# Issuing the first value columns of a fused attention and gated feed-forward kernel from the first attention result, with the value products one step earlier

## The chip, the cores and the metric

The kernel runs on one core of a Trainium2 chip. The metric is the device time of one execution in microseconds (us); the kernel before was run four times, and its median is 254.11 us. A traced execution gives the profile; all times of events below are counted from the start of that execution's span.

The engines are named as in the profile: PE is TensorE's matmul, PEld its weight load, DVE is VectorE, ACT is ScalarE, POOL is GpSimd, SP is SyncE. DMA transfers are issued by GpSimd (queue q0 in the profile) or by SyncE (queue q1), and both are carried by the same 16 DMA engines of the core.

## What is computed

The reference is an attention followed by a gated feed-forward. Batch 4, 8 heads, 768 positions, head size 64; the feed-forward goes from 512 to 1536 columns and back.

```python
scores = scale * q @ k.T + bias            # bias: -slope(head) * distance
keep = (key < 8) | ((query >= key) & (query - key < 96))
a = softmax(where(keep, scores, -1e9))
x = (a @ v)                                # heads side by side: 3072 rows of 512
out = (relu(x @ w_gate) * (x @ w_val)) @ w_out
```

Each query sees 8 global keys and at most 96 keys before it, so only a narrow band of the scores is computed.

## The kernel before

The work is cut into eight parts `s` = 0 to 7, each half a sequence (384 queries) of one batch item. For each part the attention writes `xT` (the result, transposed, 4 pieces of 128 rows, one for each pair of heads `p`), and the feed-forward of that part follows. It has 12 groups `fc` of hidden columns: `gate(fc)` makes four products with `wg` (L487) and a relu, `val(fc)` makes four products with `wv` (L500), and VectorE multiplies both (L502) into `ht`. Then `outp` multiplies `ht` by `wo_sb` (L521).

The weights come in blocks of four groups: `wg[0]`, `wv[0]` serve groups 0 to 3, and so on. In HBM they are float32; the transfers that GpSimd issues (L172, called by `load_gate` and `load_val`) convert them to bfloat16 on the way. Queries and keys come as float32 through SyncE (L131), in transfers of two heads each for parts 0 and 1: keys, then queries, for pairs 0, 1, 2, 3.

The order of the work is written out by hand: every engine runs its instructions in the order in which the Python code issues them. Parts 0 and 1 are handled apart from the others. For a pair `p` of part 1 the steps are:

- `piece_cast(1, p)` (L243 to L254): keys and queries to bfloat16, two instructions at L252 on the engine that `copy` names;
- `T(p)`, `piece_t` (L275): six transposes on TensorE (L283), then VectorE's evictions to `qT` (L288) and `kT` (L271 to L273);
- `BI(p, g)`, `piece_bias` (L336): the bias products of one of two PSUM groups;
- `SC(p, g)`, `piece_score` (L353): the score products added on top, then ScalarE's exponent (L358);
- `AW(p)`, `piece_av_wide` (L433): sums and attention products, ScalarE's logarithm and exponent (L439, L441), VectorE's product into `xT` (L444).

The list that `attention_pieces(1, fill)` returns (L465 to L468) sets their order on TensorE, and `f[0]` to `f[7]` are groups of the feed-forward of part 0 placed between them: `val(0)` to `val(3)`, `gate(4)`, `gate(5)`, `val(4)`, `val(5)`. Ahead of this list TensorE runs `gate(0)` to `gate(3)`; between the second and the third of these `piece_cast(1, 1)` is put into ScalarE's queue.

The score groups take turns in two PSUM buffers, so `BI` of a pair waits until the exponent of the pair before has read the same buffer. GpSimd's order in this stretch is at L561 to L581: memsets, `piece_cast(1, 0)`, `load_val(0)`, `load_v_half(1)` (the rest of the value rows of the first batch item, L155), `piece_cast(1, 2)`, `load_gate(1)`, memsets, `load_val(1)` and so on. In the kernel before, `piece_cast(1, 3)` is run by VectorE at the place of `C(3)` in the list of L465.

Of the kernel before, what the change touches and what calls it, by code (L numbers as in the profile page):

```python
# [15 lines left out]
def kernel(  # L16
# [12 lines left out]
    nc = tc.nc  # L29
# [82 lines left out]
    wv = [const.tile([128, N_DC, GW * 128], BF16, name=f"wv{i}") for i in range(N_FC // GW)]  # L112
# [27 lines left out]
    def load_v_globals(b):  # L140
        nc.gpsimd.dma_start(out=v_dst(b, 0, NG, 0),
                            in_=v[b, :, 0:NG, :].rearrange("h p d -> p h d"))
# [28 lines left out]
    def load_w(dst, src, f0, f1):  # L171
        nc.gpsimd.dma_start(out=dst, in_=src[:, f0:f1].rearrange("(c p) f -> p c f", p=128))  # L172

    def load_gate(i):
        load_w(wg[i], moe_w_gate, i * GW * 128, (i + 1) * GW * 128)

    def load_val(i):
        load_w(wv[i], moe_w_val, i * GW * 128, (i + 1) * GW * 128)
# [58 lines left out]
    xT_of = {}  # L237
# [5 lines left out]
    def piece_cast(s, p):  # L243
        qk = cast_pool.tile([128, 2, NN, 2, D], BF16, name="qk")
        cast_of[s, p] = qk
        for i, src in ((1, ks_of[s]), (0, qs_of[s])):
            copy = nc.gpsimd.tensor_copy
            if s == 0:
                copy = (nc.vector.tensor_copy, nc.scalar.copy, nc.scalar.copy, nc.vector.tensor_copy)[p]
            elif s == 1 and p % 2 == 1:  # L250
                copy = (nc.scalar.copy, nc.vector.tensor_copy)[p // 2]
            copy(  # L252
                qk[:, i].rearrange("t n e d -> t e n d"),
                src[:, 2 * p : 2 * p + 2, :].rearrange("t e (n d) -> t e n d", n=NN))  # L254
# [20 lines left out]
    def piece_t(s, p):  # L275
        b, half = divmod(s, 2)
        kt = kT[b % 2][p]
        qk = cast_of[s, p]
        tp = av_psum.tile([128, 512], FP32, name="av_ps")
        tp = tp[:, 0:QH].bitcast(BF16).rearrange("d (i t) -> d i t", i=2)  # L280
        for i in range(2):
            for n in range(NN):
                nc.tensor.matmul(tp[:, i, n * 128 : (n + 1) * 128],  # L283
                                 lhsT=qk[:, i, n],
                                 rhs=ident, is_transpose=True,
                                 start=(i == 0 and n == 0), stop=(i == 1 and n == NN - 1))
        if s < 2:
            nc.vector.tensor_copy(qTb[s][:, p, 0, :], tp[:, 0, :])  # L288
        else:
            for e in range(2):  # L290
                r = slice(64 * e, 64 * e + 64)
                nc.vector.tensor_copy(qTb[s % 2][r, p, e, :], tp[r, 0, :])  # L292
        put_keys(nc.vector.tensor_copy, nc.vector.tensor_copy, kt, tp[:, 1, :], half)
# [66 lines left out]
    def piece_qk(s, p, g):  # L360
        b, half = divmod(s, 2)
        kt = kT[b % 2][p]
        qd = qTb[s % 2][:, p].rearrange("d e (n p) -> d e n p", n=NN)
        bank = banks_of_half[half][g]
        cols = sum(2 * NN * w for _, _, w, _ in bank)
        ps = P["qk"].tile([128, 512], FP32, name="qk_ps")
        es = P["es"].tile([128, 480], BF16, name=f"es{g}")
        c = 0
        for j, a, w, m in bank:
            n_ = 2 * NN * w  # L370
            nc.tensor.matmul(ps[:, c : c + n_], lhsT=kt[:, j, :],  # L371
                             rhs=qd[:, :, :, a : a + w], start=True, stop=True)
            c += n_
        nc.scalar.activation(es[:, 0:cols], ps[:, 0:cols], AF.Exp, bias=0.0, scale=scale)  # L374
        c = 0
        for j, a, w, m in bank:
            n_ = 2 * NN * w
            e4 = es[:, c : c + n_].rearrange("k (e n p) -> k e n p", e=2, n=NN)
            mk = m_all[:, 2 * p : 2 * p + 2, 0 if j == 0 else 1, :, m : m + w]
            if w == WQ:  # L380
                e4 = e4.rearrange("k e n p -> k e (n p)")
                mk = mk.rearrange("k e n p -> k e (n p)")
            nc.vector.tensor_mul(e4, e4, mk)  # L383
            es_of[s, p, j] = (es, c)
            c += n_
# [33 lines left out]
    def piece_av_wide(s, p):  # L419

        todo = [t for group in first_groups[s] for t in group]
        if p % 2 == 1:
            t = P["qk"].tile([128, 2, 512], FP32, name="qk_ps")
            av = [t[:, i] for i in range(2)]
        else:
            av = [av_psum.tile([128, 512], FP32, name="av_ps") for _ in range(2)]
        for what in range(2):
            av3 = av[what][:, 0:QH].rearrange("d (n p) -> d n p", n=NN)
            for i, (j, a, w, m) in enumerate(todo):
                es, c = es_of[s, p, j]  # L430
                for e in range(2):
                    z0 = D + 2 * D * (2 * p + e)
                    nc.tensor.matmul(av3[64 * e : 64 * e + 64, :, a : a + w],  # L433
                                     lhsT=ones if what == 0 else vbuf[0][:, j, z0 : z0 + D],
                                     rhs=es[:, e, c : c + NN * w].rearrange("k (n p) -> k n p", n=NN),
                                     start=(i == 0), stop=(i == len(todo) - 1),
                                     skip_group_check=True)
        ln = rc_pool.tile([128, QH], FP32, name="lnd")
        nc.scalar.activation(ln, av[0][:, 0:QH], AF.Ln, bias=0.0, scale=1.0)  # L439
        rc = rc_pool.tile([128, QH], FP32, name="rcp")  # L440
        nc.scalar.activation(rc, ln, AF.Exp, bias=0.0, scale=-1.0)  # L441
        if s not in xT_of:
            xT_of[s] = xt_pool.tile([128, N_DC, QH], BF16, name="xT")
        nc.vector.tensor_tensor(xT_of[s][:, p, :], av[1][:, 0:QH], rc, op=ALU.mult)  # L444

    def attention_pieces(s, fill=()):
        T = lambda p: [(0.34, lambda: piece_t(s, p))]
        QK = lambda p: [(0.18, lambda g=g: piece_qk(s, p, g)) for g in range(3)]
        AW = lambda p: [(0.58, lambda: piece_av_wide(s, p))]
        C = lambda p: [(0.0, lambda: piece_cast(s, p))]  # L450
        BI = lambda p, *gs: [(0.2, lambda g=g: piece_bias(s, p, g)) for g in gs]
        SC = lambda p, *gs: [(0.2, lambda g=g: piece_score(s, p, g)) for g in gs]
        X = lambda *fs: [(0.0, f) for f in fs]
        if s == 0:
            return (C(0) + X(lambda: load_v_globals(0), lambda: load_v(0, 0), lambda: load_v(0, 1),
                             lambda: load_v(0, 2), lambda: load_v(0, 3), lambda: load_gate(0))
                    + C(1) + T(0) + BI(0, 0, 1) + C(2) + T(1) + SC(0, 0, 1) + BI(1, 0) + SC(1, 0) + C(3) + T(2)
                    + BI(1, 1) + SC(1, 1) + BI(2, 0) + T(3) + X(lambda: copy_v_globals(0, 1, 4), lambda: load_qk_after(1, nc.vector, True))
                    + SC(2, 0) + BI(2, 1) + SC(2, 1)
                    + BI(3, 0) + SC(3, 0) + BI(3, 1) + SC(3, 1)  # L460
                    + AW(0) + AW(1) + AW(2)
                    + AW(3) + X(second_pools, lambda: warm(4)))
        if s == 1:
            f = [[x] for x in fill]
            return (T(0) + BI(0, 0, 1) + T(1) + SC(0, 0, 1) + C(3) + BI(1, 0) + SC(1, 0)  # L465
                    + BI(1, 1) + SC(1, 1) + T(2) + BI(2, 0) + SC(2, 0) + f[0] + T(3) + BI(2, 1) + SC(2, 1)
                    + f[1] + BI(3, 0) + SC(3, 0) + f[2] + BI(3, 1) + SC(3, 1) + f[3] + AW(0) + AW(1) + f[4]
                    + AW(2) + f[5] + f[6] + AW(3) + f[7])  # L468
        AV = lambda p: [(0.29, lambda e=e: piece_av(s, p, e)) for e in range(2)]
        g = QK(3)  # L470
        a = AV(2)
        return (QK(0) + QK(1) + AV(0) + QK(2) + AV(1) + g[0:1] + a[0:1] + g[1:2] + a[1:2] + g[2:3]
                + [(0.0, lambda: None)] * 2 + AV(3))
# [88 lines left out]
    copy_v_globals(0, 4, NT)  # L562
    for p in range(HP):
        nc.gpsimd.memset(kT[0][p][:, 6, NG + 48 : 128].bitcast(mybir.dt.uint32), 0)
    piece_cast(1, 0)
    load_val(0)
    load_v_half(1)
    piece_cast(1, 2)
    load_gate(1)
    for p in range(HP):  # L570
        nc.gpsimd.memset(kT[1][p][:, 3, 32:128].bitcast(mybir.dt.uint32), 0)
        nc.gpsimd.memset(kT[1][p][:, 6, NG + 48 : 128].bitcast(mybir.dt.uint32), 0)
# [87 lines left out]
```

## Time and profile before

| what | us |
|---|---|
| four runs | 253.53, 253.57, 254.65, 254.88 |
| median | 254.11 |
| the profiled execution | 253.53 |
| its span | 251.8 |
| TensorE busy in the span | 240.2 |
| VectorE, ScalarE, GpSimd busy | 134.9, 157.7, 88.9 |

The span is counted from the first to the last instruction of the traced execution; its own time has a little more around it. The granted clock of TensorE is full in all slices. Busy shares are means over the whole span: what a change of one stretch is worth is read from that stretch. The chain of work is followed back from the last instruction, at each step to what released it. A releaser is inferred from semaphore events and can be wrong where two things ended close together.

In the stretch of the change, the first gate products start at 17.83 us, the first transposes of part 1 at 20.53, the first value products at 26.15, and the first `AW` of part 1 at 31.12.

### The profile page before, as it was taken

To read this page: it belongs to the slowest core of one execution; us is meant where nothing else is said; L and a number is where in the kernel's file an instruction comes from. 1 tells how busy PE (TensorE), PEld (TensorE's weight loads), DVE (VectorE), ACT (ScalarE), POOL (GpSimd) and SP (SyncE) were. 2 spreads that over 40 slices of the span, in tenths; PEclk is the share of its full clock that TensorE was granted. 3 is DMA by queue.
4 is the path that set the end of the run, shared out by engine and by line. 5 is a ranking of instruction groups with operands and counts; after the bars stand their busy time and mean duration, and the time that the engine had idled before them with its cause. 6 is when DMAs were issued, how large, how long until landed. Compare 5 with 4: busy or idle time off the path is not lost.

```text
span 251.8 us, 4919 instructions
## 1 busy us (share of the span) xinstructions
PE 240.2 (95%) x1753; PEld 143.8 (57%) x1763; DVE 134.9 (54%) x340; ACT 157.7 (63%) x318; POOL 88.9 (35%) x211
## 2 busy tenths in 40 slices
PE   6878999999999999999999999999999999999994
PEld 2556665655555566556565566556565566555643
DVE  3845564695555557617762567517762657524410
ACT  6777565726675687656785687656785687553312
POOL 7709983700476526702537067202530000000000
PEclk9999999999999999999999999999999999999999
DMA  6999999990889994859367976729361200020012
GB/s 186 150 258 166 187 183 243 199 156 6 249 160 222 181 254 95 126 108 289 90 104 76 235 194 149 47 89 288 89 103 48 77 3 1 0 99 29 0 44 84
DMA packets 77704, 33.15 MB, mean 132 GB/s; under 512 B 53488, under 2 KB 74736, under 8 KB 77680
## 3 DMA queue, kind: packets, MB, share of 16 engines
q1 hardware_dynamic: 45824, 24.93, 37.3%
q0 software_dynamic: 31856, 7.91, 32.4%
q8 instruction: 14, 0.23, 0.4%
q14 instruction: 10, 0.08, 0.1%
HBM read 28.38 MB, written 6.29 MB: 138 GB/s over the span
## 4 chain that ended last, share of the span: by engine, by line
PE 80%; DVE 6%; DMA 4%; ACT 4%; POOL 3%; issue 2%; POOLq 0%; ACTq 0%; DVEq 0%
PE ff_ps L521 24%; PE ff_ps L500 22%; PE ff_ps L487 21%; PE av_ps L399 5%; PE qk_ps L371 4%; DMA wg<-in_moe_w_gate_dram 3%; DVE xT L416 2%; DVE ht L502 2%; POOL vbuf L155 1%; ACT grelu L493 1%; ACT rcp L413 1%; ACT lnd L408 1%; PE qk_ps L336 1%; PE av_ps L283 1%; DVE qT L292 1%
## 5 line engine op out<-in xcount | busy, mean ns | idle before, releaser
L500 PE MATMUL ff_ps<-xT,wv 128*128 128x384 bf16 x384 | 78.1, 326 | 1.5 <-ACT grelu L493 0.6
L487 PE MATMUL ff_ps<-xT,wg 128*128 128x384 bf16 x384 | 77.7, 326 | 1.3 <-DMA wg<-in_moe_w_gate_dram 0.9
L502 DVE TENSOR_TENSOR ht<-ff_ps,grelu 128x384 bf16<-128x384 f32 x96 | 54.2, 565 | 24.5 <-PE ff_ps L500 20.9
L493 ACT ACTIVATE grelu<-ff_ps 128x384 bf16<-128x384 f32 x94 | 46.0, 490 | 33.6 <-PE ff_ps L487 18.8
L521 PE MATMUL ff_ps<-wo_sb,ht 128*128 128x512 bf16 x267 | 63.9, 379 | 0.5
L416 DVE TENSOR_TENSOR xT<-av_ps,rcp 64x384 bf16<-64x384 f32 x48 | 26.7, 555 | 45.0 <-ACT rcp L413 44.2
L487 PEld LDWEIGHTS <-wg 128*128 128x128 bf16 x384 | 36.1, 97 | 24.6 <-DMA wg<-in_moe_w_gate_dram 1.4
L500 PEld LDWEIGHTS <-wv 128*128 128x128 bf16 x384 | 36.0, 97 | 24.5 <-issue 3.5
L383 DVE TENSOR_TENSOR es<-es,m_all 128x432 bf16<-128x432 bf16 (+5 forms) x108 | 34.0, 343 | 22.2 <-ACT es L374 21.7
L374 ACT ACTIVATE es<-qk_ps 128x432 bf16<-128x432 f32 (+2 forms) x72 | 38.0, 529 | 10.1 <-PE qk_ps L371 8.2
L521 PEld LDWEIGHTS <-ht 128*128 128x128 bf16 x276 | 25.9, 97 | 26.8
L296 POOL CAST kc<-ks 128x384 bf16<-128x384 f32 x20 | 9.9, 539 | 59.2 <-DMA ks<-in_k_dram 59.2
L408 ACT ACTIVATE lnd<-av_ps 64x384 f32<-64x384 f32 x48 | 23.3, 486 | 11.6 <-PE av_ps L399 11.0
L526 ACT COPY osb<-ff_ps 128x512 f32<-128x512 f32 x23 | 13.5, 587 | 23.3 <-PE ff_ps L521 20.6
L371 PE MATMUL qk_ps<-qT,kT 128*128 128x432 bf16 (+5 forms) x108 | 24.8, 286 | 0.0
L155 POOL DMA_DIRECT2D vbuf<-in_v_dram x28 | 24.4, 877 | 0.6 <-issue 0.6
L399 PEld LDWEIGHTS <-vbuf 128*128 128x128 bf16 x216 | 18.0, 98 | 7.4
L399 PE MATMUL av_ps<-es,vbuf 128*128 128x216 bf16 (+4 forms) x216 | 20.9, 226 | 0.0
L371 PEld LDWEIGHTS <-kT 128*128 128x128 bf16 x108 | 10.6, 98 | 7.7 <-issue 0.2
L304 POOL CAST qz<-qs 128x192 bf16<-128x192 f32 x40 | 12.6, 364 | 3.6 <-DMA qs<-in_q_dram 3.3
L358 ACT ACTIVATE es<-qk_ps 128x864 bf16<-128x864 f32 (+3 forms) x16 | 10.6, 709 | 4.5 <-PE qk_ps L353 4.5
L413 ACT ACTIVATE rcp<-lnd 128x384 f32<-128x384 f32 x24 | 12.6, 525 | 0.8
(81 smaller groups left out, 151.8 us busy)
## 6 DMA issues: line engine op xcount, KB each, us to landing
out_dram<-osb SPq DMA_DIRECT2D x23, 256.0 KB
ks<-in_k_dram SPq DMA_DIRECT2D x5, 768.0 KB
qs<-in_q_dram SPq DMA_DIRECT2D x5, 768.0 KB
vbuf<-in_v_dram POOLq DMA_DIRECT2D x24, 120.0 KB, 5.0
ks<-in_k_dram SPq DMA_DIRECT2D x12, 192.0 KB
qs<-in_q_dram SPq DMA_DIRECT2D x12, 192.0 KB
wg<-in_moe_w_gate_dram POOLq DMA_DIRECT2D x3, 512.0 KB, 7.1
wv<-in_moe_w_val_dram POOLq DMA_DIRECT2D x3, 512.0 KB, 7.6
```

The lines of the kernel that those rows point to most:

```text
L155: nc.gpsimd.dma_start(out=v_dst(b, NG + r0, NG + r0 + n, j), in_=v[b, :, KT * j + r0 : KT * j + r0 + n, :].rearrange("h p d -> p h d"))
L371: nc.tensor.matmul(ps[:, c : c + n_], lhsT=kt[:, j, :], rhs=qd[:, :, :, a : a + w], start=True, stop=True)
L374: nc.scalar.activation(es[:, 0:cols], ps[:, 0:cols], AF.Exp, bias=0.0, scale=scale)
L383: nc.vector.tensor_mul(e4, e4, mk)
L399: nc.tensor.matmul(av3[:, :, a : a + w], lhsT=vb[:, j, z0 : z0 + 128], rhs=es[:, c : c + NN * w].rearrange("k (n p) -> k n p", n=NN), star ...
L408: nc.scalar.activation(ln[o0 : o0 + 64], av[d0 : d0 + 64, 0:QH], AF.Ln, bias=0.0, scale=1.0)
L416: nc.vector.tensor_tensor(xT_of[s][r, p, :], av_of[s, p, e_][r, 0:QH], rc[r], op=ALU.mult)
L487: nc.tensor.matmul(psg[:, 0:QH], lhsT=w_of(wg, dc, fc), rhs=xT[:, dc, :], start=(dc == 0), stop=(dc == N_DC - 1))
L493: nc.scalar.activation(gr, psg[:, 0:QH], AF.Relu, bias=0.0, scale=1.0)
L500: nc.tensor.matmul(psv[:, 0:QH], lhsT=w_of(wv, dc, fc), rhs=xT[:, dc, :], start=(dc == 0), stop=(dc == N_DC - 1))
L502: nc.vector.tensor_tensor(ht[:, fc, :], psv[:, 0:QH], st[fc], op=ALU.mult)
L521: nc.tensor.matmul(ps2, lhsT=ht[:, fc, n * 128 : (n + 1) * 128], rhs=wo_sb[:, fc, :], start=(fc == 0), stop=(fc == N_FC - 1))
```

## The change

Three edits, all in the start-up of part 1:

- GpSimd copies one element of `xT` of part 0 (pair 0) into one element of `wv[0]`, and `load_val(0)` follows at once, ahead of `piece_cast(1, 0)`. The transfer overwrites that element. So the columns are issued once the first of the four result pieces is written, and no longer after the cast of pair 0.
- `piece_cast(1, 3)` goes from VectorE to GpSimd, behind `load_gate(1)`. `C(3)` leaves the list.
- The value groups `f[0]` to `f[2]` stand elsewhere in the list: `f[0]` ahead of `T(2)` (it stood behind `SC(2, 0)`), `f[1]` behind `SC(2, 0)` (it stood behind `SC(2, 1)`), `f[2]` behind `SC(2, 1)` (it stood behind `SC(3, 0)`). `f[3]` stays behind `SC(3, 1)`.

```diff
@@ piece_cast
             if s == 0:
                 copy = (nc.vector.tensor_copy, nc.scalar.copy, nc.scalar.copy, nc.vector.tensor_copy)[p]
-            elif s == 1 and p % 2 == 1:
-                copy = (nc.scalar.copy, nc.vector.tensor_copy)[p // 2]
+            elif s == 1 and p == 1:
+                copy = nc.scalar.copy
@@ attention_pieces, s == 1
-            return (T(0) + BI(0, 0, 1) + T(1) + SC(0, 0, 1) + C(3) + BI(1, 0) + SC(1, 0)
-                    + BI(1, 1) + SC(1, 1) + T(2) + BI(2, 0) + SC(2, 0) + f[0] + T(3) + BI(2, 1) + SC(2, 1)
-                    + f[1] + BI(3, 0) + SC(3, 0) + f[2] + BI(3, 1) + SC(3, 1) + f[3] + AW(0) + AW(1) + f[4]
+            return (T(0) + BI(0, 0, 1) + T(1) + SC(0, 0, 1) + BI(1, 0) + SC(1, 0) + BI(1, 1) + SC(1, 1)
+                    + f[0] + T(2) + BI(2, 0) + SC(2, 0) + f[1] + T(3) + BI(2, 1) + SC(2, 1) + f[2] + BI(3, 0)
+                    + SC(3, 0) + BI(3, 1) + SC(3, 1) + f[3] + AW(0) + AW(1) + f[4]
                     + AW(2) + f[5] + f[6] + AW(3) + f[7])
@@ GpSimd's order
-    piece_cast(1, 0)
+
+    nc.gpsimd.tensor_copy(wv[0][0:1, 0, 0:1], xT_of[0][0:1, 0, 0:1])
     load_val(0)
+    piece_cast(1, 0)
     load_v_half(1)
     piece_cast(1, 2)
     load_gate(1)
+    piece_cast(1, 3)
```

More of the change, by code (lines that the diff above doesn't have):

```diff
@@ L564 @@
         nc.gpsimd.memset(kT[0][p][:, 6, NG + 48 : 128].bitcast(mybir.dt.uint32), 0)
+    nc.gpsimd.tensor_copy(wv[0][0:1, 0, 0:1], xT_of[0][0:1, 0, 0:1])
+    load_val(0)
     piece_cast(1, 0)
-    load_val(0)
     load_v_half(1)
```

## The prediction

> **What bounds the kernel now.** I read the page first (busy shares, slices, chain), then the waits of TensorE, then the timelines of TensorE, GpSimd and VectorE between 10 and 40 us, and last the two DMA queues in windows of 2 us.
>
> The page's first lines and the head of its chain:
>
> ```profile
> PE 240.2 (95%) x1753; PEld 143.8 (57%) x1763; DVE 134.9 (54%) x340; ACT 157.7 (63%) x318; POOL 88.9 (35%) x211
> PE   6878999999999999999999999999999999999994
> PE 80%; DVE 6%; DMA 4%; ACT 4%; POOL 3%; issue 2%; POOLq 0%; ACTq 0%; DVEq 0%
> ```
>
> TensorE is the bound, and from the fifth slice on it has work nearly all the time. Since its queue runs in the written order, a stall put into it early is carried to the end, and only a stall taken out of it is won. So the question is which stalls lie in the stretch that the change touches. The waits of TensorE between 17 and 41 us, all of them:
>
> ```profile
> PE ff_ps L487 <- DMA wg<-in_moe_w_gate_dram: 0.9, 1, 0.9
> PE qk_ps L336 <- ACT es L358: 0.8, 1, 0.8
> PE ff_ps L500 <- ACT grelu L493: 0.6, 1, 0.6
> PE qk_ps L353 <- DVE kT L271: 0.4, 1, 0.4
> ```
>
> None is a wait for value columns, value products or the casts that are moved. After 64 us there is one more kind, 0.4 us in all. The most that can be won here is 0.8+0.6+0.4 = 1.8 us; the gate wait ends before the change acts.
>
> GpSimd's timeline, with the start, the duration and in brackets the idle time before:
>
> ```profile
> 10.94 0.36 POOL L564 MEMSET kT<- 128x36 uint32 x4
> 18.57 0.50 POOL L252 CAST qk<-ks 128x384 bf16<-128x384 f32 x1 [7.28 <-PE ff_ps L487]
> 19.06 0.51 POOL L252 CAST qk<-qs 128x384 bf16<-128x384 f32 x1
> 19.51 0.77 POOL L172 DMA_DIRECT2D wv<-in_moe_w_val_dram  x1
> 20.27 2.50 POOL L155 DMA_DIRECT2D vbuf<-in_v_dram  x3
> ```
>
> The 7.28 us is put down to a gate product, but the code orders this cast before any gate; it waits for the key rows of part 1, so these land at about 18.5. The first value columns wait behind it, leave at 19.51 and, with 5.7 us from issue to landing in the view of that tile, are there at 25.2. TensorE reads them at 26.15: 0.9 us of margin, and no wait.
>
> TensorE's timeline where the work sits:
>
> ```profile
> 17.83 2.86 PE L487 MATMUL ff_ps<-xT,wg 128*128 128x384 bf16 x16 [0.88 <-DMA wg<-in_moe_w_gate_dram]
> 20.53 0.50 PE L283 MATMUL av_ps<-ident,qk 128*128 128x128 bf16 x6
> ...
> 24.52 0.51 PE L283 MATMUL av_ps<-ident,qk 128*128 128x128 bf16 x6
> 24.93 0.51 PE L336 MATMUL qk_ps<-dd,sid 128*128 128x216 bf16 x4
> 25.79 0.42 PE L353 MATMUL qk_ps<-qT,kT 64*128 64x216 bf16 x4 [0.35 <-DVE kT L271]
> 26.15 0.82 PE L500 MATMUL ff_ps<-xT,wv 128*128 128x384 bf16 x4
> ```
>
> Four gates, then the first transposes at 20.53, for which the casts of pair 0 are ready at 19.57 (19.06 + 0.51): 0.96 us of cover. Pair 1 is cast on ScalarE from 19.73 to 20.68 and transposed at 21.48: 0.80 us.
>
> Last, the queues. q0 carries GpSimd's transfers, q1 SyncE's. The rows are the windows 16 to 18 (first two), 18 to 20, and 36 to 38 us (last two): packets, MB, share of 16 engines.
>
> ```profile
> q1 hardware_dynamic: 841, 0.61, 93.9%
> q0 software_dynamic: 36, 0.03, 10.3%
> ...
> q1 hardware_dynamic: 802, 0.58, 95.8%
> ...
> q0 software_dynamic: 261, 0.26, 79.1%
> q1 hardware_dynamic: 207, 0.15, 33.0%
> ```
>
> From 16 to 20 us the DMA engines are full with the queries and keys of part 1 alone. The 36 packets on q0 are the rest of the first gate columns (landing 17.78 in the chain): at about 0.1 us a packet, some two of the 16 engines still hold them, and have not yet come to the keys.
>
> **What the Trainium skill says.** "DMA: Bandwidth & Descriptors", § Queues, rings and completion order: each DMA engine takes turns between the queue rows that have work, a packet at a time. The window 36 to 38 agrees when both queues are loaded (261 to 207). The start of the queries' load doesn't: issued from 11.91 on, it shows no packet from 12 to 14, while 659 packets of q0 ran. So the rule is not the whole of it. "TensorE: Matmul & The Clock Gate", § Architectural detail: VectorE and ScalarE run strictly in order. The timelines agree. "SBUF — State Buffer", § Who interferes with whom: a VectorE cast in a two-port mode and a GpSimd instruction shut each other out. A GpSimd cast beside VectorE's takes 0.72 us, alone 0.51.
>
> **The change part by part.**
>
> *Issue of the first value columns.* The one-element copy waits for the first of four result pieces (L444, 14.36 + 0.56 = 14.92). GpSimd is idle then. Copy 0.1 us (as its small memsets), so the issue runs from about 15.1 to 15.9, 4.4 us earlier. In the old place the packets began to come 1.5 to 2.4 us after the issue (46 on q0 from 20 to 22 us, 333 from 22 to 24). So they now come at 16.6 to 17.5, in the middle of the load of queries and keys.
>
> *What that meets.* Each engine owes the columns 32 packets (512 KB in 1 KB packets over 16). At 104 ns (333 packets, 108.5% of 16 engines over 2 us) this is 3.3 us. A query or key transfer (192 KB) is 16 packets of 768 B and a completion per engine, 36 ns each (841 packets, 93.9%): 0.6 us. The last engine is free of gate columns at 17.78. Before, it then did keys 0 (18.4) and queries 0 (19.0). With turns, both transfers of pair 0 and the 32 packets share it: 17.78 + 3.3 + 1.2 = 22.3. Queries 0 land 3.3 us late. The cast follows to 22.85, the transposes start at 22.9 instead of 20.53: 2.4 us. Pair 1 follows at 23.5, is cast on ScalarE to 24.0 and transposed at about 24.05 instead of 21.48: 2.5 us, which contains the 2.4. From below: if the engine finishes what stood in q1 first, 0, and not less, since the key load can't be helped by more traffic. Above: 3.3, if the margins are used up by something else. I take 2.5.
>
> *Two casts from VectorE to GpSimd.* VectorE loses 0.70 + 0.65 us, run from 22.88 to 24.15. It then stood idle 0.91 us before the next transposes came, so nothing is won. GpSimd gains 1.0 to 1.2 us. Behind it stand eight memsets, the second value columns (issued 25.70, landing 7.6 us later at 33.3, first used by the fifth value group at 34.74) and the rest. The value rows and gate columns ahead of them keep q0 loaded to 30.7, so a later issue is hidden up to about 1.4 us; with TensorE itself late by 2.5, there is more cover. Without cover it would cost at most 1.2. I take 0. The second gate columns leave up to 0.7 us earlier, or late with the casts; they had 1.7 us of margin.
>
> *Value products one step earlier.* Four groups of four products, 0.65 us each, are the same number. The first now stands before the transposes of pair 2. VectorE takes its product (0.47 us to the next start) before the evictions that the score at L353 waits for. First product to VectorE took 0.93 us, transposes to VectorE 0.54. Counted from the product's start, VectorE is free at 0.93 + 0.47 = 1.40; the transposes, 0.65 later, would have had it at 1.19. The eviction is 0.2 us late, and the 0.4 wait becomes 0.6. With pipelining I book 0.25. The other three groups keep 1.4 us or more between a bank's exponent and its reuse: 0. The columns themselves land at 22.3 on this reckoning, before they are needed: 0.
>
> *Later.* The next queries (part 2) are ready for transposes 4 us ahead (cast of pair 0 ends 42.4, transposes 46.95), so no delay of GpSimd's queue up to that reaches TensorE, and no stage gives the loss back.
>
> **Sum.** 2.5 + 0.25 = about 2.75 us. The profiled execution took 253.53 us (span 251.8 and 1.7 around it): 256.3. It was the fastest of the four; from their median 254.11 it is 256.9. I forecast 256.5.
>
> **Rivals.** *Queries first.* The engines finish q1's backlog, as they finished the gate columns before the first key packet. Then the value columns come after the last engine's queries (the old load ended at about 22.3): 22.3 + 3.3 = 25.6, against a need at 24.6: 0.3 to 1.0 us, plus 0.25. Time 254.3 to 255.4. For it: the empty q1 from 12 to 14. Against: 36 to 38 us.
>
> *A gain.* One mechanism: an early value product takes the place of a wait. The places are 23.20 (0.8 us, exponent) and 25.79 (0.4). It decides if value products fill both at once, which gives 252.4 to 252.9. Against: the written order has no value product ahead of the first place, and ahead of the second the product delays the same evictions.
>
> *The change does not do what it says.* Had the copy to wait for the fourth result piece (17.72), the issue would end at 18.7, packets would come from 19.5 on, and only the last pairs, cast 2 us before use, would be met. Time 254.0 to 254.8. The built program sets the wait at the first piece, which speaks against it.
>
> **Chances and range.** Differences under 0.5% (1.27 us) are about what cannot be told from no change. Collision 0.56 (nearly all slower), queries first 0.26 (mostly within), no effect of the issue 0.10 (within), gain 0.08. So faster 0.08, same 0.34, slower 0.58. The collision's own range is 255.4 to 257.6; the range to hold 8 in 10 reaches down through the second case, 254.0 to 257.6.
>
> **What would show it.** Value columns issued near 15.1 and landing near 22; GpSimd's cast of queries 0 ending near 22.8 instead of 19.6; a wait of about 2.4 us ahead of the first transposes; the wait at L353 grown to about 0.6. I am wrong if the first transposes still start at 20.5 (then queries first, and a wait ahead of the first value product), or if the wait at L336 shrinks.

## The result and the profile after

The changed kernel takes 254.24 us (median of 35 runs, 252.9 to 256.0); beside it, on the same chip, the kernel before took 253.63 us (56 runs, 252.3 to 256.3; the 254.11 of the first part is the median of four of them). The medians stand 0.6 us apart; the ratio of the comparison is 1.0014 with a 95% interval of 1.0000 to 1.0027, which is a loss of 0 to 0.7 us. That is within what I had called no change. I had forecast a loss of 2.75 us.

The profiled execution of the changed kernel took 252.90 us and was its shortest run; the one of before took 253.53, near its median. So the two traces show where things moved, but not by themselves what the median pays. The page's lines that answer to those of before, busy time, TensorE's slices and the head of the chain:

```profile
PE 240.8 (96%) x1753; PEld 144.5 (58%) x1763; DVE 132.3 (53%) x338; ACT 157.6 (63%) x318; POOL 90.4 (36%) x214
PE   7978998999999999999999999999999999999994
PE 81%; DVE 6%; DMA 6%; ACT 4%; issue 1%; SPq 0%; POOL 0%; ACTq 0%; DVEq 0%
```

The chain holds 6% of DMA instead of 4%, and in its list by line a new entry, the transfer of the value columns with 4%. TensorE's waits between 17 and 41 us (who waits, for whom, us in total, times, longest):

```profile
PE qk_ps L336 <- ACT es L358: 0.8, 1, 0.8
PE qk_ps L353 <- DVE kT L271: 0.6, 1, 0.6
PE ff_ps L500 <- ACT grelu L493: 0.6, 1, 0.6
PE ff_ps L487 <- DMA wg<-in_moe_w_gate_dram: 0.4, 1, 0.4
```

There is no wait ahead of the transposes (L283). The wait at L353 grew from 0.4 to 0.6. TensorE's timeline (start, duration, and in brackets the idle time before with its releaser):

```profile
17.34 3.03 PE L487 MATMUL ff_ps<-xT,wg 128*128 128x384 bf16 x16 [0.40 <-DMA wg<-in_moe_w_gate_dram]
20.20 0.50 PE L283 MATMUL av_ps<-ident,qk 128*128 128x128 bf16 x6
...
23.96 0.30 PE L353 MATMUL qk_ps<-qT,kT 64*128 64x168 bf16 x6
24.39 0.82 PE L500 MATMUL ff_ps<-xT,wv 128*128 128x384 bf16 x4
25.05 0.50 PE L283 MATMUL av_ps<-ident,qk 128*128 128x128 bf16 x6
25.39 0.51 PE L336 MATMUL qk_ps<-dd,sid 128*128 128x216 bf16 x4
26.52 0.42 PE L353 MATMUL qk_ps<-qT,kT 64*128 64x216 bf16 x4 [0.62 <-DVE kT L271]
```

The scores at 23.96 are followed after 0.43 us, where in the kernel before the next work followed the same scores after 0.24 (24.28 to 24.52). The missing 0.2 us is a wait too short to be listed: the trace has the last packets of the columns landing at 24.34, just ahead of 24.39. GpSimd's timeline shows the early issue:

```profile
14.75 0.18 POOL L566 COPY wv<-xT 1x1 bf16<-1x1 bf16 x1 [3.32 <-DVE xT L444]
15.23 0.77 POOL L172 DMA_DIRECT2D wv<-in_moe_w_val_dram  x1 [0.30 <-POOL wv L566]
18.04 0.60 POOL L252 CAST qk<-ks 128x384 bf16<-128x384 f32 x1 [2.04 <-PE ff_ps L487]
18.59 0.50 POOL L252 CAST qk<-qs 128x384 bf16<-128x384 f32 x1
...
24.64 0.51 POOL L252 CAST qk<-qs 128x384 bf16<-128x384 f32 x1 [0.88 <-DMA qs<-in_q_dram]
```

The casts of pair 0 are not late, but earlier than before by 0.5 us. The last cast, of queries 3, now waits for its data. The two queues in the windows 16 to 18, 18 to 20 and 20 to 22 us (packets, MB, share of 16 engines; two rows each):

```profile
q1 hardware_dynamic: 911, 0.66, 102.4%
q0 software_dynamic: 24, 0.02, 6.9%
...
q0 software_dynamic: 211, 0.22, 64.6%
q1 hardware_dynamic: 463, 0.33, 52.1%
...
q0 software_dynamic: 257, 0.25, 74.7%
q1 hardware_dynamic: 305, 0.23, 41.8%
```

The columns were issued at 15.23, and yet from 16 to 18 us the engines carried 911 packets of q1 and 24 of q0, and these 24 are the end of the gate columns (landing 17.29). By the packets in the trace, the first one of the value columns came at 18.40, 3.17 us after the issue. In the kernel before it came at 20.99, 1.48 us after the issue, and in the four other traces with the late issue 1.47 to 1.54 us after it; with the early issue it was 1.96 to 3.31 us. So the longer delay belongs to the early issue, and isn't the time that every such transfer needs to start. Once the columns had begun, the queues did share the engines: 257 packets to 305 from 20 to 22 us.

The time at which the last of the 16 engines finished each transfer, from the completions in the trace (the third column is an experiment below):

| transfer | before | after | columns issued first |
|---|---|---|---|
| gate columns 0 | 17.78 | 17.29 | 17.23 |
| keys 0, queries 0 | 18.41, 19.01 | 17.91, 18.48 | 21.01, 22.25 |
| keys 2, queries 2 | 20.69, 21.24 | 20.18, 20.89 | 23.98, 24.52 |
| keys 3, queries 3 | 21.80, 22.34 | 23.11, 24.59 | 25.14, 25.64 |
| value columns 0 (issued at) | 25.23 (19.51) | 24.34 (15.23) | 22.00 (10.53) |

After the change SyncE issued queries 2 at 14.72 and keys 3 at 15.30, the columns between them at 15.23. All that was issued earlier lands as it did before, relative to the gate columns; only keys 3 and queries 3, issued after the columns, are late, by 1.8 and 2.7 us on that count.

Where the 0.63 us between the two spans lie: gate products start 0.49 earlier, with the gate columns' landing; gates to first transposes +0.16 (a wait of 0.2 to 0.3 us of this place comes and goes between executions, with the last `xT` piece); first transposes to first attention products of part 1 +0.40 (10.59 to 10.99, the 0.2 on the columns and 0.2 at L353); then nothing up to the transposes of part 2; from these to the first product at L521 −0.69; the rest −0.02. The −0.69 is a meeting of two engines. VectorE's copies of `kT` in part 2, first of before, then of after:

```profile
48.99 1.64 DVE L269 COPY kT<-kT 128x56 bf16<-128x56 bf16 x1
```

```profile
49.06 0.85 DVE L269 COPY kT<-kT 128x56 bf16<-128x56 bf16 x1
```

The same copy in the next pair takes 0.18 us. GpSimd's two zeroings of the part 2 buffers (L603 before, L606 after) ran from 47.89 to 50.60 and from 47.18 to 49.88; in both the copy ends when they end (50.63, 49.91). So VectorE is shut out for the rest of the zeroing, and how long that is depends on when the queries of part 2 land, which start it.

### The profile page after: what moved, and what is told of

The parts are those of the page before. It is cut to its first block, busy times and chain, and to the rows that moved or that the text cites. A ratio compares the mean times of both kernels' runs of the same rounds, so it can differ in the third digit from the quotient of the medians.

```text
span 251.1 us, 4919 instructions
## 1 busy us (share of the span) xinstructions
PE 240.8 (96%) x1753; PEld 144.5 (58%) x1763; DVE 132.3 (53%) x338; ACT 157.6 (63%) x318; POOL 90.4 (36%) x214
## 4 chain that ended last, share of the span: by engine, by line
PE 81%; DVE 6%; DMA 6%; ACT 4%; issue 1%; SPq 0%; POOL 0%; ACTq 0%; DVEq 0%
PE ff_ps L521 24%; PE ff_ps L500 23%; PE ff_ps L487 21%; PE av_ps L399 5%; PE qk_ps L371 4%; DMA wv<-in_moe_w_val_dram 4%; DVE xT L416 2%; DVE ht L502 2%; PE av_ps L283 2%; ACT grelu L493 1%; DMA qs<-in_q_dram 1%; ACT rcp L413 1%; PE qk_ps L336 1%; ACT lnd L408 1%; PE qk_ps L353 1%
## 5 line engine op out<-in xcount | busy, mean ns | idle before, releaser
L502 DVE TENSOR_TENSOR ht<-ff_ps,grelu 128x384 bf16<-128x384 f32 x96 | 53.4, 557 | 27.3 <-PE ff_ps L500 22.2
L521 PE MATMUL ff_ps<-wo_sb,ht 128*128 128x512 bf16 x267 | 63.9, 379 | 0.5
L383 DVE TENSOR_TENSOR es<-es,m_all 128x432 bf16<-128x432 bf16 (+5 forms) x108 | 33.4, 337 | 22.7 <-ACT es L374 22.2
L521 PEld LDWEIGHTS <-ht 128*128 128x128 bf16 x276 | 25.8, 97 | 26.8
## 6 DMA issues: line engine op xcount, KB each, us to landing
out_dram<-osb SPq DMA_DIRECT2D x23, 256.0 KB
```

Of the source, the lines that this page charges most:

```text
L502: nc.vector.tensor_tensor(ht[:, fc, :], psv[:, 0:QH], st[fc], op=ALU.mult)
L521: nc.tensor.matmul(ps2, lhsT=ht[:, fc, n * 128 : (n + 1) * 128], rhs=wo_sb[:, fc, :], start=(fc == 0), stop=(fc == N_FC - 1))
```

## The experiments

Unless an expectation says otherwise, nothing of the computation is left out. "Medians" are of the kernel and of the kernel before on the same chip in the same session; "first transposes to attention" is the interval that is 10.59 us before and 10.99 after.

**One part at a time.** The early issue alone, in the kernel before:

```diff
+    nc.gpsimd.tensor_copy(wv[0][0:1, 0, 0:1], xT_of[0][0:1, 0, 0:1])
+    load_val(0)
     piece_cast(1, 0)
-    load_val(0)
```

> The kernel before with only the early issue of the first value columns (element copy and issue ahead of the cast of pair 0); the list and the casts are as before. Order of issue (transfers are carried about in the order in which they were issued, whatever their queue): the columns, issued near 15, follow the query transfer of pair 2 and land near 24.3; keys and queries of pairs 0 to 2 land as before, so the first transposes start at 20.2 to 20.5 and the stretch from them to the first attention products of part 1 stays at 10.6 us (before: 10.59). Value rows, later columns and the next queries move 0.5 us earlier, so the wait of VectorE for GpSimd's memsets (L603) is 0.8 us instead of 1.6. Time 0.3 to 0.7 us below before. Turns (my prediction's collision): first transposes near 22.9, time 2.5 us above.

Measured 254.02 against 253.44 us, ratio 1.0040 (1.0012 to 1.0067). The first transposes have no wait, as expected, and the interval to the attention stays 10.59; but the time, expected 0.3 to 0.7 us below, came out above. The profiled execution does not show why: it took 254.00 us, but its span of 251.6 is no longer than the 251.8 of the kernel before. VectorE shows how near a loss is:

```profile
24.13 0.59 DVE L252 CAST qk<-qs 128x384 bf16<-128x384 f32 x1 [0.63 <-DMA qs<-in_q_dram]
25.12 0.36 DVE L288 COPY qT<-av_ps 128x384 bf16<-128x384 bf16 x1 [0.39 <-PE av_ps L283]
```

Queries 3 landed at 24.11 instead of 22.34. Their cast still stands in VectorE's queue ahead of the evictions of pair 2, and 0.39 us was left. In this trace a landing later than about 24.5 would have held the evictions, and with them the scores at L353. In later profiles with the early issue queries 3 landed at 24.63 to 27.28, though the transposes of pair 2 were also later in most of them.

The order of the value products alone, columns and casts as before:

```diff
-   ... + SC(1, 1) + T(2) + BI(2, 0) + SC(2, 0) + f[0] + T(3) + BI(2, 1) + SC(2, 1) + f[1] + BI(3, 0) + SC(3, 0) + f[2] + BI(3, 1) ...
+   ... + SC(1, 1) + f[0] + T(2) + BI(2, 0) + SC(2, 0) + f[1] + T(3) + BI(2, 1) + SC(2, 1) + f[2] + BI(3, 0) + SC(3, 0) + BI(3, 1) ...
```

> The kernel before with only the three value groups one step earlier in the list; columns issued as before, cast of pair 3 on VectorE. The columns land at 25.2 as before, but are wanted at about 24.6: a wait of 0.6 us, and the eviction of the transposes of pair 2 behind the first product, 0.2 us more. Stretch from first transposes to first attention products of part 1: 11.4 us (before 10.59, changed kernel 10.99). Time 0.5 to 0.9 us above before. If the eviction order is not what costs in the changed kernel, only the wait for the columns shows: 11.2.

Measured 254.71 against 253.44 us, 1.0060 (1.0036 to 1.0083), more than the 0.5 to 0.9 us expected. First transposes to attention 11.37, as expected. TensorE's timeline has both parts of the price:

```profile
25.26 0.82 PE L500 MATMUL ff_ps<-xT,wv 128*128 128x384 bf16 x4 [0.52 <-DMA wv<-in_moe_w_val_dram]
...
27.39 0.42 PE L353 MATMUL qk_ps<-qT,kT 64*128 64x216 bf16 x4 [0.61 <-DVE kT L271]
```

The casts of pair 3 on GpSimd alone:

```diff
-            elif s == 1 and p % 2 == 1:
-                copy = (nc.scalar.copy, nc.vector.tensor_copy)[p // 2]
+            elif s == 1 and p == 1:
+                copy = nc.scalar.copy
@@ the list: C(3) left out
@@ GpSimd's order
     load_gate(1)
+    piece_cast(1, 3)
```

> The kernel before with only the cast of pair 3 moved from VectorE to GpSimd, behind the issue of the second gate columns. VectorE was idle where the cast stood, so the stretch stays at 10.6 us. GpSimd's later issues come about 1.1 us later; the queries of part 2 land later by up to that, and the memsets behind their casts end later: the wait of VectorE for them grows from 1.6 towards 2.4 us. Time 0 to 0.8 us above before. If later issues don't matter: no change.

Measured 253.73 against 253.44 us, 1.0015 (0.9996 to 1.0035), interval 10.59: alone it costs nothing that can be told.

**Does the order of issue decide?** The changed kernel without the copied element, its columns issued right behind the first gate columns, ahead of all keys:

```diff
-    nc.gpsimd.tensor_copy(wv[0][0:1, 0, 0:1], xT_of[0][0:1, 0, 0:1])
-    load_val(0)
@@ attention_pieces(0, ...)
-        lambda: load_gate(0)
+        lambda: load_gate(0), lambda: load_val(0)
```

> The changed kernel with the first value columns issued right behind the first gate columns (near 10.6), without the element copy, so ahead of the keys of part 1 (issued from 12 on). Order of issue: every engine carries these 32 packets (3.3 us) before the first keys; keys 0 and queries 0 land near 21 to 22 instead of 18.5, first transposes near 22.5 to 23, time 2 to 2.7 us above the changed kernel. Turns: keys share with the columns and land at 20 to 22 too, but the columns land after 20 and not before 20.5 on all engines. If transfers don't get into each other's way at all: first transposes at 20.3 and no change.

Measured 255.21 against 253.44 us (4 runs), 1.0091 (1.0059 to 1.0123); the trace is of the longest of the four, 256.89. TensorE, and the queues from 16 to 18 and from 18 to 20 us:

```profile
17.27 3.11 PE L487 MATMUL ff_ps<-xT,wg 128*128 128x384 bf16 x16
22.86 0.51 PE L283 MATMUL av_ps<-ident,qk 128*128 128x128 bf16 x6 [2.48 <-POOL qk L252]
```

```profile
q0 software_dynamic: 292, 0.30, 88.4%
q1 hardware_dynamic: 179, 0.14, 27.4%
...
q1 hardware_dynamic: 648, 0.47, 75.6%
q0 software_dynamic: 136, 0.12, 37.5%
```

In its start-up this is what I had forecast for the change: first transposes at 22.9, 2.5 us of wait for the casts of pair 0, queries 0 landing at 22.3. The median pays less, 1.8 us more than the kernel before. The collision needs the columns to be issued ahead of the keys. Issued behind the keys and queries of pairs 0 to 2, the same bytes leave pair 0 alone.

**Does the meeting of VectorE and GpSimd matter in the median?** The two zeroings moved ahead of the casts of part 2, so that they run at 38 to 42 us, in the kernel before, in the changed kernel, and with the early issue alone:

```diff
+    for i in range(2):
+        nc.gpsimd.memset(qz[1 - i]...)
     for p in range(HP):
         piece_cast(2, p)
-    for i in range(2):
-        nc.gpsimd.memset(qz[1 - i]...)
```

> The kernel before with GpSimd's two memsets of qz (L603) moved ahead of the four casts of part 2, into a stretch in which GpSimd waits 3.7 us for keys. Lock (VectorE's copy at L269 is shut out while these memsets run): the copy takes 0.2 us in every case instead of 1.6, and the stretch from the transposes of part 2 to the first output products is 16.75 us instead of 17.44. Time 0.3 to 0.7 us below before. If the long copy has another cause, it stays long and the time is the same.

> The changed kernel with the same move of the two memsets. If the changed kernel owes its near-equality to a shorter wait for the memsets, this one is slower than the kernel before with the memsets moved by the full loss at the start, 0.4 to 0.5 us (0.15 to 0.2%), and faster than the changed kernel by 0.2 to 0.4. If the two effects are unrelated, the difference of the two is as small as that of changed and before, 0.36 us or less.

> The kernel before with the early issue of the value columns, and the two memsets moved. The early issue alone came out 1 us slower in its time, with the start stretch unchanged and a profile that shows a late first attention and a 0.5 us longer wait at 94 us. Chance of phases[...]: time within 0.3 us of the kernel before with memsets moved. A cost of the early issue itself: 0.5 to 1 us above it.

Measured against 253.44 us: 253.24, ratio 0.9995 (0.9981 to 1.0009); 254.08, 1.0022 (1.0007 to 1.0037); 254.13, 1.0023 (1.0003 to 1.0043). The meeting itself is gone; the copy in the kernel before with early zeroings:

```profile
49.67 0.18 DVE L269 COPY kT<-kT 128x56 bf16<-128x56 bf16 x1
```

The interval from the transposes of part 2 to the first L521 is 16.76 us there, against 17.44. But the medians don't show that 0.7 us, and the two kernels are no closer than without the edit (0.84 us apart, 0.61 before it). So the meeting explains why the traced pair differs by −0.63, not the median's difference. The trace of the changed kernel with early zeroings shows what can: there the columns were issued at 16.76 and landed at 26.48, and TensorE waited 1.2 us for them ahead of the first value product (first transposes to attention 12.06). It is of a run of 255.55 us, 1.5 above the median of its kernel, so it shows the place of a loss and not its usual size.

**The first value product behind the transposes of pair 2**, in the changed kernel:

```diff
-                    + f[0] + T(2) + BI(2, 0) + SC(2, 0) + f[1]
+                    + T(2) + f[0] + BI(2, 0) + SC(2, 0) + f[1]
```

> The changed kernel with the first value product behind the transposes of pair 2 (ahead of their bias products). Eviction order: VectorE takes the transposes first and the product covers the wait ahead of the score products of pair 2, so the wait of 0.6 at L353 goes to 0 to 0.1; the product is wanted 0.35 us later, so the columns (landing 24.3) are in time. Stretch from first transposes to first attention products of part 1: 10.2 to 10.4 us (changed 10.99, before 10.59). Time 0.5 to 0.7 us below changed. If the order of evictions isn't the cause, 10.8 to 11.0.

Measured 253.19 against 253.44 us, 0.9996 (0.9975 to 1.0017). TensorE:

```profile
25.18 0.51 PE L283 MATMUL av_ps<-ident,qk 128*128 128x128 bf16 x6 [0.21 <-POOL qk L252]
25.52 0.81 PE L500 MATMUL ff_ps<-xT,wv 128*128 128x384 bf16 x4
26.17 0.51 PE L336 MATMUL qk_ps<-dd,sid 128*128 128x216 bf16 x4
26.62 0.35 PE L353 MATMUL qk_ps<-qT,kT 64*128 64x216 bf16 x4
```

Here the product runs while VectorE evicts pair 2, the wait at L353 is gone, and the columns, landing at 25.09, are in time for 25.52. The interval to the attention is 10.31, 0.28 below before and 0.68 below the changed kernel, although this trace has its own 0.21 us of wait for the cast of pair 2. The times alone don't settle it: the interval reaches above 1 and overlaps that of the changed kernel (1.0000 to 1.0027). The 0.21 us also shows that a transfer issued shortly ahead of the columns can be late. Here SyncE issued queries 2 at 15.35 and GpSimd the columns at 15.60, and queries 2 landed at 24.56, 3.3 us later than in the kernel before.

**Early issue together with the casts**, value products in the old order (the first and third diff above in one kernel):

> The kernel before, with the early issue of the first value columns and with the pair 3 casts of part 1 on GpSimd; the value products stay in the old order. The early issue alone came out 0.4% slower (254.02 us), the casts alone 0.15% (253.73 us). In the profile of the early issue alone, queries 3 landed at 24.11 instead of 22.34, and VectorE, whose cast of queries 3 stands ahead of the evictions of pair 2 in its queue, had only 0.39 us left (24.72 to 25.12); in a second profile with the early issue queries 3 landed at 27.28 and TensorE waited 2.3 us at L353. Theory A (the late pair 3 blocks VectorE's queue): with the casts on GpSimd the evictions run free, the wait at L353 is 0.4 us again, first transposes to attention weights 10.59 us, and the time is 253.3 to 253.7 us. Theory B (the early issue costs by its start-up or by a later lock of VectorE against GpSimd): 254.0 us or more, as with the early issue alone.

Measured 253.65 against 253.41 us, 1.0016 (0.9991 to 1.0041). The time is in theory A's range, but the interval overlaps that of the early issue alone. The trace says more. GpSimd and TensorE:

```profile
24.68 0.51 POOL L252 CAST qk<-qs 128x384 bf16<-128x384 f32 x1 [0.33 <-DMA qs<-in_q_dram]
```

```profile
26.28 0.42 PE L353 MATMUL qk_ps<-qT,kT 64*128 64x216 bf16 x4 [0.35 <-DVE kT L271]
```

Queries 3 landed at 24.63 and GpSimd waited for them, with no eviction of pair 2 behind the cast, and L353 waits no longer than in the kernel before. The second profile that the expectation names, of the early issue with early zeroings, shows the blocking itself: with queries 3 landing at 27.28, VectorE's cast of them ran from 27.30, the evictions of pair 2 behind it from 27.78, and TensorE waited 2.3 us at L353. Its run was the longest of its kernel, 257.15 us, so the size is not used. That the casts' move is what lets the early issue pass is thus in accord with the traces, not settled by the times.

**A gate group into the exponent's wait.** The fourth gate group (0.65 us) goes from ahead of the attention into the 0.8 us at L336, in the changed kernel and in the kernel before:

```diff
-    for i in (4, 6):
-        f1_0[i][1]()
-    for _, f in attention_pieces(1, [f1_0[i] for i in (1, 3, 5, 7, 8, 10, 9, 11)]):
+    f1_0[4][1]()
+    for _, f in attention_pieces(1, [f1_0[i] for i in (1, 3, 5, 7, 8, 10, 9, 11, 6)]):
@@ the list
-            return (T(0) + BI(0, 0, 1) + T(1) + SC(0, 0, 1) + BI(1, 0) ...
+            return (T(0) + BI(0, 0, 1) + T(1) + SC(0, 0, 1) + f[8] + BI(1, 0) ...
```

> The changed kernel, with the fourth gate group (0.65 us of TensorE) taken from ahead of the attention and put into the wait for the exponent at L336 (0.82 us). First transposes then start 0.65 us earlier relative to the gates, and the wait at L336 is about 0.2 us. Theory A (the early columns land just as they are needed, at 24.3 against 24.39): the first value product, now due at about 23.7, waits for its columns for what the gate has won, and the time stays at 254.0 to 254.3 us, with a wait of 0.6 to 0.9 us on the columns. Theory B (the columns have room): 253.4 to 253.6 us and no such wait.

Measured 254.23 against 253.41 us, 1.0035 (1.0019 to 1.0050): theory A's time. TensorE:

```profile
22.39 0.82 PE L487 MATMUL ff_ps<-xT,wg 128*128 128x384 bf16 x4
23.27 0.51 PE L336 MATMUL qk_ps<-dd,sid 128*128 128x216 bf16 x4
...
25.79 0.82 PE L500 MATMUL ff_ps<-xT,wv 128*128 128x384 bf16 x4 [1.13 <-DMA wv<-in_moe_w_val_dram]
```

The exponent's wait is filled, and 1.13 us of wait for the columns (landing at 25.75) stand in its place, more than the 0.6 to 0.9 expected.

> The same move of the fourth gate group, in the kernel before. There the columns land at 25.2 and the first value product was due at 26.15, now at about 25.5. Casts of pair 0 were ready at 19.57 (first transposes then at 19.9 instead of 20.53), of pair 1 at 20.68 (transposes at 20.83). Theory A (stalls taken out of TensorE's queue are won as long as nothing lands too late): the wait at L336 falls from 0.8 to about 0.2, and the time by 0.65 to 252.7 to 252.9 us. Theory B (the loads of part 1 are the bound of the stretch, and the transposes wait for what they have been moved ahead of): 253.2 to 253.5 us, with a wait ahead of the transposes.

Measured 253.51 against 253.41 us, 1.0004 (0.9990 to 1.0018): theory B's time, but not for its reason. There is no wait ahead of the transposes; in this execution the first attention came late, and columns issued at 18.64 landed at 26.73:

```profile
26.77 0.50 PE L500 MATMUL ff_ps<-xT,wv 128*128 128x384 bf16 x2 [0.42 <-DMA wv<-in_moe_w_val_dram]
```

So in this execution even the kernel before had no room in its columns for a start 0.65 us earlier.

**All together**: the changed kernel with three of these edits (product behind, gate in the wait, early zeroings).

> The changed kernel with the first value product behind the transposes of pair 2 instead of ahead of them, the fourth gate group in the exponent's wait, and the two zeroings of the part 2 buffers moved ahead of the casts of part 2. Worked out from the runs so far: the product behind the transposes takes 0.4 to 0.6 us out of the wait at L353 (253.19 us measured with it), the gate 0.65 us. The first value product is due about 4.6 us after the first transposes, at 24.2 to 24.9, with columns landing at 24.3 to 25.1. Theory A (columns land just as needed): a wait of up to 0.7 us ahead of the first value product takes most of the gate's gain, time 252.9 to 253.2 us. Theory B (columns have room): 252.4 to 252.7 us.

Measured 252.75 against 253.41 us, ratio 0.9970 (0.9950 to 0.9990): the only version whose interval lies below 1. Its median is between the two theories' ranges. TensorE:

```profile
20.16 0.51 PE L283 MATMUL av_ps<-ident,qk 128*128 128x128 bf16 x6 [0.45 <-POOL qk L252]
...
22.15 0.82 PE L487 MATMUL ff_ps<-xT,wg 128*128 128x384 bf16 x4
23.04 0.51 PE L336 MATMUL qk_ps<-dd,sid 128*128 128x216 bf16 x4
...
25.12 0.82 PE L500 MATMUL ff_ps<-xT,wv 128*128 128x384 bf16 x4 [0.25 <-DMA wv<-in_moe_w_val_dram]
```

The columns' wait is down to 0.25 us, and part of what the gate left is now lost ahead of the transposes, to the cast of queries 0. In this trace the loads are the next bound of the stretch.

## Why the prediction was wrong

The forecast was 256.5 us, a loss of 2.75; measured is a loss of 0 to 0.7, inside the range given but not what was forecast. The rival "queries first" (254.3 to 255.4, a wait of 0.3 to 1.0 us for the columns and 0.25) comes nearest to what happened, though the columns landed at 24.34 and not at 25.6.

- *Issue of the first value columns*: right. Issued at 15.23 (forecast 15.1), 4.3 us earlier. The copy took 0.18 us and not 0.1, and the issue waited 0.30 for it.
- *What that meets*: this step failed, and with it 2.5 of the 2.75 us. I let the columns' packets begin 1.5 to 2.4 us after the issue, at 16.6 to 17.5, and from there take turns with the keys and queries of pair 0, by the rule that I quoted from the Trainium skill, "DMA: Bandwidth & Descriptors", § Queues, rings and completion order. What failed is when the turns begin. In the trace the first packet of the columns came at 18.40, when the transfers of pair 0 were all but through (17.91 and 18.48 on the last engine); the 911 packets to 24 before that are no turns. From 20 to 22 us, 257 packets to 305, the trace agrees with the rule, but the columns now shared the engines with keys 3 and queries 3. Why their packets began later than in the old place is not shown. With the columns issued ahead of all keys the collision came about as sized (2.48 us of wait in that trace), so its place was wrong. I had seen the contrary evidence, the queries' queue empty from 12 to 14 us while older gate columns ran, and gave it 26%. The window that I took for turns, 36 to 38 us, doesn't show which transfers had been issued when. One more gap: the page's packet is a group of descriptors, typically 9 to 17; that it is one packet of the profile I assumed, and no run here shows it.
- *The columns land at 22.3, before they are needed: 0*: wrong, from the same step. They land 8.6 to 9.7 us after their issue in all profiles with this early issue, at 24.3 to 26.5, because the issue itself moves with the first attention (15.2 to 16.8). They are needed about 4.0 us after the first transposes, at 24.2 in the traced run of the changed kernel, its shortest, and at 25.3 in the trace of the same kernel with early zeroings. That gives 0.2 us of wait in the first and 1.2 in the second. How much the median run waits was not measured; the median's loss leaves room for some tenths.
- *The eviction behind the value product*, 0.2 to 0.25: right. The wait at L353 is 0.62 in the changed kernel and 0.61 with the order alone.
- *Two casts from VectorE to GpSimd: 0*: right by themselves (1.0015, from 0.9996 to 1.0035). What I missed is what they may do together with the early issue: the step looked at VectorE's idle time before, not at queries 3 landing 2 us later in front of its evictions.
- *No stage gives the loss back*: wrong for the traced pair, where 0.7 us came back at 49 us. I had looked at casts against transposes, and not at VectorE's copy beside GpSimd's zeroing. "SBUF — State Buffer", § Who interferes with whom, which I had used for casts alone, covers it: a VectorE copy in a two-port mode and a GpSimd instruction shut each other out, whole instruction by whole instruction. The traces agree in the main, 1.64 and 0.85 us for a copy of 0.18, ending with the zeroing; that this copy runs in such a mode they don't show. Nor was the hold one instruction long: in the kernel before the copy came at 48.99, during the first zeroing (to 49.28), and was held through the second (49.21 to 50.60) as well. In the medians it was not to be seen.
- *A gain*, rival with 8%: the changed kernel has none, but its places were named rightly. The kernel with three edits fills both waits, with a gate group and a value product, and takes 252.75 us; I had put that case at 252.4 to 252.9. The early zeroings are part of it too, so how much the filled waits give is not shown.

## What to carry to other kernels

When a transfer is issued earlier, look first at what has been issued before it on all queues: in these traces it left the transfers issued well before it alone, and shared the engines with those issued from shortly before it on (queries 2, 0.25 us ahead of it, landed 3.3 us late). These are the ones whose users to check. A move that makes data land just in time has no slack to give: here a stall of 0.8 us filled ahead of it came back as 1.13 us of wait for that data. And put filler work where an eviction or an exponent is being waited for, not ahead of the work that this eviction follows: in the traces, the same product cost 0.2 us in front of the transposes and won 0.3 behind them.

## What was unexpected of the hardware

- Over two queues on the same 16 engines, landing followed the order of issue closely: columns issued at 10.53 landed at 22.00, ahead of queries 0 (issued 12.91, landing 22.25); issued at 15.23, behind queries 2 (14.72, landing 20.89) and ahead of queries 3 (16.76, landing 24.59), they landed at 24.34. It is not strict: keys 0, issued at 12.49, landed at 21.01, before the columns issued at 10.53. Once begun, the value columns took about equal turns with the other queue (257 packets to 305 from 20 to 22 us), so what differs is when they begin, 3.17 us after the issue here and 1.48 in the kernel before. What sets that was not tried.
- A VectorE copy of 0.18 us lasted 2.12 us beside GpSimd's zeroing in the kernel that issued the columns first (51.09 to 53.80), and TensorE waited 0.47 us for VectorE at 53.90.
